# A mixer of local attention and a gated MLP on one core: new order lists for all five engines

## The chip, the core and the metric

The kernel runs on one core of one Trainium2 chip. A core has TensorE (PE in the profile; PEld is its weight load), VectorE (DVE), ScalarE (ACT), GpSimd (POOL) and SyncE (SP, which here only issues DMAs). Each works through its own list of instructions in order, and semaphores hold an instruction back until what it needs is done. The metric is the device time of one execution in microseconds (us).

## What is computed

x has 2048 rows of 512. It is layer-normalized; branch A is attention with 32 heads of 16 in which each row looks at itself and seven rows behind it, two apart; branch B is a gated MLP whose gate is mixed over the rows by a 2048 x 2048 matrix. The output is the sum of x and both.

```python
def _A_ref(x, wqkv, wo):
    B, S, D = x.shape
    H = 32
    Dh = D // H
    W, dil = (8, 2)
    qkv = (lambda x, *d: x.transpose(*d))((x @ wqkv).reshape(B, S, 3, H, Dh), 2, 0, 3, 1, 4)
    q, k, v = (qkv[0], qkv[1], qkv[2])
    scale = Dh ** (-0.5)
    pos = jnp.arange(S)
    off = jnp.arange(W) * dil
    idx = pos[:, None] - off[None, :]
    mask = idx >= 0
    ...
    logits = jnp.einsum('bhsd,bhswd->bhsw', q, kg) * scale
    logits = jnp.where(mask[None, None, :, :], logits, -1000000000.0)
    attn = _softmax(logits, axis=-1)
    o = jnp.einsum('bhsw,bhswd->bhsd', attn, vg)
    return (lambda x, *d: x.transpose(*d))(o, 0, 2, 1, 3).reshape(B, S, D) @ wo

def _B_ref(x, w_in, w_sp, b_sp, w_out):
    ...
    z = _gelu(jnp.einsum('bsd,df->bsf', x, w_in))
    z1 = z[..., :Fh].copy()
    z2 = _layernorm(z[..., Fh:], axis=-1)
    g = jnp.einsum('ts,bsf->btf', w_sp, z2) + b_sp[None, :, None]
    return jnp.einsum('bsf,fd->bsd', z1 * g, w_out)
x = A_x
xn = _layernorm(x, axis=-1)
return x + _A_ref(xn, A_wqkv, A_wo) + _B_ref(xn, B_w_in, B_w_sp, B_b_sp, B_w_out)
```

Fh is 896 here: F is 1792.

## The kernel before

The program is a set of named tasks. Each task belongs to one engine, names what it reads and writes, and holds one instruction, or on PE a run of matmuls. Waits are made from the reads and writes: a task waits for the last writer of what it reads, and for writer and readers of what it overwrites. A planner puts the tasks of each engine into a list, and `plan.orders` (L1244) gives that list by name: for each engine, each name stands behind the one before it. So the order on every engine is written out in full, and the planner's estimates have no say in it. An engine never passes over a waiting task.

The tasks, by stage. Numbers in names are blocks b of 128 rows (0 to 15), groups j of four blocks (0 to 3), weight columns c (0 to 3) or output tiles t (0 to 7, each two blocks, from the last blocks to the first).

- Normalizing x: `ldx` (a DMA, L588) brings a block into one of eight slots. `bnst` (L650) and `bnag` (L653) on DVE make mean and variance, `rstd` on POOL takes the power -0.5 (L655), `norm` on DVE applies both (L665), and `xTd` (L669, a transposing DMA issued by SP) puts the block into the transposed x, xnT. Blocks 0 to 3 are transposed on PE instead. norm of block b waits also for the transpose of block b-4, whose buffer it takes.
- q and k: `Q` and `K` (L733) on PE, 4 matmuls of 512 columns each, into a pair of PSUM banks; `QKe` (L741) on ACT evicts the pair, `halo` (L747) copies the 16 columns that the next group needs. `ldq` and `ldk` (L605) bring the weights.
- Logits: `prod` (L757) on DVE multiplies q with eight shifted k, 128 x 4096 elements; `padd` (L762) adds such products up over c. `lg` (L772) on PE sums over the 16 elements of a head with the mask hm as weights, and so waits for the last padd of its group (padd0_2 for lg0) and for hm, which POOL builds with `hm0`, `hm1`, `hm2` (L569 to L573). `lge` (L794) evicts, `smask` (L799) masks the first rows with what `mask0` and `mask1` (L576, L577) made, `pT` (L803) transposes all four groups by DMA after the last one.
- Softmax of group j: `sm1`, `sm2`, `sm3`, `ssub` (L810 to L820, DVE), `sexp` (L823, ACT), `sz1`, `sz2`, `sz3`, `srec`, `sattn` (L830 to L842, DVE).
- Branch B's halves: `z2` (L852, before it L875 for blocks 0 to 3) and `z1` (L895) on PE, 8 matmuls of 448 columns; `z2g` and `z1g` are their Gelu on ACT (L858, L882, L901). `z2s` (L907) squares z2 on ACT; DVE makes mean and variance of four blocks at a time with `zm`, `zq`, `ze`, `zv` (L915 to L924), POOL the power `zr` (L926), DVE `zb` (L928), and `zn` normalizes z2: on ACT for blocks 0 to 11 (L933), on DVE for 12 to 15 (L937). `T1` to `T4` (L954, DVE) are sums and differences of normalized blocks.
- v: `V` (L717) on PE needs the whole of xnT, `Ve` (L721) evicts on ACT.
- The mixing by w_sp in a seven-product scheme. For tile t, `w` (L962) loads the transposed weights by DMA into one of two slots, `S13`, `S2`, `S4` (L974, L978, L980, DVE) make sums of them, and `P1` to `P7` (L1015, PE) are eight matmuls of 448 columns each. `cA`, `cB`, `cE` (L1030) copy between PSUM banks on ACT, `g11` and `g21` (L1033) evict on ACT, `g12` (L1057) and `g22` (L1061) on DVE. P4 adds on into the bank that g22 reads, so P4 of a tile waits for its g22. `u` (L1039) multiplies with z1 and `uT` (L1041) transposes by DMA.
- Attention's output: `pv` (L1145), `pva` (L1149), `pvc` (L1153) on DVE, with v shifted down by partitions through `Vhaloa`, `Vhalob`, `Vzero` (L1122, L1125, DMAs), and `OTd` (L1157), a transposing DMA.
- Output: `out` (L1207 for branch A, L1211 for B, PE), `os` (L1202) and `fin` (L1220, L1219) around it, then the store.

Slot 0 of the `w` weights lies over the slots of blocks 0 to 3 and over their normalized copies, so w0_0 waits for norm8 to norm11 and w0_1 for xTd12 to xTd15 to have landed. Slot 1 lies over xnT, so w1 waits for the last V.

Of the kernel before, what the change touches and what calls it, by code (L numbers as in the profile page):

```python
# [1353 lines left out]
```

## Time and profile before

| what | value |
|---|---|
| median of 3 runs | 228.32 us (227.99 to 229.19) |
| the profiled execution, its time | 228.66 us |
| its span, first to last instruction | 226.9 us |
| mean granted TensorE clock | 1.00 |
| PE busy up to 13.15 us / from there to 125.88 / to 224.67 | 12.26 of 13.15 / 111.39 of 112.73 (DVE 111.03) / 98.75 of 98.79 |
| longest wait in total | POOL for DVE, 33.4 us in 3 waits |

A row of the profile has the start in us, the length in us, the engine, the line of the code, the operation, what it writes and reads, and how many instructions are merged in it. What stands in brackets is the time for which the engine was idle before it, and what ended that. A PE row's length holds a modelled end that reaches some 0.16 us into the next row, so that gaps on PE are read from the distance of starts. Merged rows of other engines can overlap by 0.1 us for the same reason.

### The profile page before, as it was taken

Reading aid. Unit: us, or ns where it says so; the run is one execution under the profiler, and the core shown is the slowest. Engines: PE = TensorE matmul, PEld = TensorE weight load, DVE = VectorE, ACT = ScalarE, POOL = GpSimd, SP = SyncE. Lnnn points to the kernel's source line nnn. Section 1 sums busy time; section 2 is a strip of 40 time slices with the busy share of each in tenths; the row PEclk is TensorE's granted clock in tenths of the full one; section 3 lists DMA queues with packets and bytes.
Section 4 is the critical chain, followed back from the end, with each engine's and each line's share of the span. In section 5 each row is a group of like instructions: output and inputs, shape, how many; then the busy total and the mean of one; then the engine's idle time right before and its main releaser. Section 6 shows DMA issues by size and latency. Waiting matters only on the chain.

```text
span 226.9 us, 3133 instructions
## 1 busy us (share of the span) xinstructions
PE 222.4 (98%) x1176; PEld 121.7 (54%) x1176; DVE 210.3 (93%) x255; ACT 134.2 (59%) x241; POOL 35.5 (16%) x35
## 2 busy tenths in 40 slices
...
GB/s 220 271 159 162 72 25 28 81 329 97 0 3 0 0 0 161 141 143 261 226 196 138 192 193 86 203 82 221 232 103 141 98 167 144 198 114 130 46 127 92
DMA packets 77400, 29.96 MB, mean 132 GB/s; under 512 B 68669, under 2 KB 75339, under 8 KB 77259
## 3 DMA queue, kind: packets, MB, share of 16 engines
q1 hardware_dynamic: 74250, 25.08, 53.6%
...
q8 instruction: 9, 0.15, 0.3%
...
## 4 chain that ended last, share of the span: by engine, by line
PE 44%; DVE 40%; POOL 6%; issue 5%; DMA 4%; ACT 0%; POOLq 0%; DVEq 0%
PE ps L1015 27%; DVE arena L757 13%; PE ps L1211 11%; DVE arena L762 7%; POOL fpool L655 6%; PE ps L1207 6%; DMA arena<-in_A_x_dram 4%; DVE arena L954 4%; DVE fpool L650 2%; DVE arena L1145 2%; DVE arena L974 2%; DVE arena L1149 1%; DVE arena L978 1%; DVE arena L820 1%; DVE arena L839 1%
## 5 line engine op out<-in xcount | busy, mean ns | idle before, releaser
L1015 PE MATMUL ps<-arena 128*128 128x448 f16 (+1 forms) x448 | 86.9, 353 | 0.8 <-DVE arena L978 0.7
L1015 PEld LDWEIGHTS ps<-arena 128*128 128x128 f16 (+1 forms) x448 | 43.5, 98 | 42.8 <-DVE arena L978 1.2
L757 DVE TENSOR_TENSOR arena<-arena 128x4096 bf16<-128x4096 bf16 x16 | 36.2, 2280 | 0.0
L1145 DVE TENSOR_TENSOR arena<-arena 128x4096 bf16<-128x4096 bf16 x16 | 36.0, 2277 | 0.0
L1030 ACT ACTIVATE ps<-ps 128x448 f32<-128x448 f32 x16 | 8.5, 529 | 44.4 <-PE ps L1015 25.4
L733 PE MATMUL ps<-arena 128*128 128x512 bf16 x128 | 28.5, 380 | 0.0
L1149 DVE TENSOR_TENSOR arena<-arena 128x4096 bf16<-128x4096 bf16 (+1 forms) x16 | 27.8, 1739 | 0.0
L762 DVE TENSOR_TENSOR arena<-arena 128x4096 bf16<-128x4096 bf16 x12 | 27.4, 2284 | 0.0
L1211 PE MATMUL ps<-arena 128*128 128x512 bf16 (+2 forms) x126 | 27.1, 356 | 0.0
L895 PE MATMUL ps<-arena 128*128 128x448 bf16 x128 | 24.8, 353 | 0.0
L655 POOL TENSOR_TENSOR fpool<-fpool 128x1 f32<-128x1 f32 x16 | 21.1, 1321 | 15.3 <-DVE fpool L653 14.2
L1220 ACT ACTIVATE arena<-ps 128x512 bf16<-128x512 f32 (+2 forms) x17 | 9.5, 562 | 21.1 <-PE ps L1211 21.1
L895 PEld LDWEIGHTS ps<-arena 128*128 128x128 bf16 x128 | 18.4, 145 | 6.2 <-issue 0.4
L733 PEld LDWEIGHTS ps<-arena 128*128 128x128 bf16 x128 | 14.3, 114 | 13.7 <-issue 0.8
L852 PE MATMUL ps<-arena 128*128 128x448 bf16 x96 | 19.2, 353 | 0.0
L1211 PEld LDWEIGHTS ps<-arena 128*128 128x128 bf16 x126 | 11.9, 98 | 12.4
L926 POOL TENSOR_TENSOR fpool<-fpool 128x4 f32<-128x4 f32 x4 | 12.2, 3048 | 38.5 <-DVE fpool L924 33.4
L741 ACT ACTIVATE arena<-ps 128x1024 bf16<-128x1024 f32 x16 | 16.1, 1018 | 2.5 <-PE ps L733 2.5
L1207 PE MATMUL ps<-arena 128*128 128x512 bf16 (+2 forms) x72 | 16.8, 356 | 0.0
L1033 ACT ACTIVATE arena<-ps,fpool 128x448 bf16<-128x448 f32 x16 | 10.0, 633 | 11.0 <-PE ps L1015 11.0
L907 ACT ACTIVATE arena<-arena 128x896 bf16<-128x896 bf16 x16 | 15.2, 950 | 0.1
L901 ACT ACTIVATE arena<-ps 128x896 bf16<-128x896 f32 x16 | 14.5, 922 | 0.5 <-PE ps L895 0.4
...
## 6 DMA issues: line engine op xcount, KB each, us to landing
...
arena<-arena SPq DMA_TRANSPOSE x40, 3.2
```

The costliest lines, as they stand in the source:

```text
L655: T("pool", lambda g: g.tensor_tensor(Fv("rstd", 1, b), Fv("mv", 1, 2 * b + 1), Fv("mhalf", 1), ALU.pow), reads=[("mv", b), "mhalf"], writ ...
L733: last = t.matmul(bank(k + which), AC(off["wqk"] + 1024 * dc + col0, [[4, 128]]), AC(off["xnT"] + dc * S + 512 * j, [[1, 512]]), start=(dc ...
L741: T("act", lambda a: a.activation(AC(qo, [[ko - qo, 2], [1, 512]]), ps[:, 512 * k: 512 * k + 1024].rearrange("p (t n) -> p t n", t=2), ACT ...
L757: T("dve", lambda v: v.tensor_tensor(pbv, qb, kb, ALU.mult), reads=[("QT", c, j), ("KT", c, j), ("KTpad", c, j)], writes=[("pb", s_)], est ...
L762: T("dve", lambda v: v.tensor_tensor(A("pb", 4096, 4096 * a), A("pb", 4096, 4096 * a), A("pb", 4096, 4096 * b), ALU.add), reads=[("pb", b) ...
L852: last = t.matmul(ps[:, 512 * (k + hf): 512 * (k + hf) + HF], AC(off["xnT"] + dc * S + 128 * b, [[1, 128]]), AC(off["w_in2"] + FH * dc + H ...
L895: lastm = t.matmul(ps[:, 512 * (k + hf): 512 * (k + hf) + HF], AC(off["xnT"] + dc * S + b, [[NTOK, 128]]), AC(off["w_in1"] + FH * dc + HF ...
L1015: last = t_.matmul(pb_(k_), st(k), mv(k), start=(start and k == 0), stop=(k == 7), skip_group_check=True)
L1145: T("dve", (lambda iv, tv, av: lambda v: v.tensor_tensor(tv, iv, av, ALU.mult))(iv, tv, av), reads=[("attn", q // 4)] + [("V", i_) for i_ ...
L1149: T("dve", (lambda n: lambda v: v.tensor_tensor(AC(off["Vs"], [[4096, 2], [1, n]]), AC(off["Vs"], [[4096, 2], [1, n]]), AC(off["Vs"] + n, ...
L1207: t_.matmul(po, AC(off["OT"] + 1024 * (t % 3) + 512 * r_ + 128 * cc, [[1, 128]]), AC(off["wo"] + 512 * cc + c0, [[1, n]]), start=False, st ...
L1211: last = t_.matmul(po, AC(off["z1"] + FH * tb + 128 * fc, [[1, 128]]), AC(off["w_out"] + 512 * fc + c0, [[1, n]]), start=False, stop=(fc = ...
```

## The change

All five lists in `plan.orders` are replaced; no task is added, removed or altered. On DVE the norms of blocks 8 to 15 come at other places, each with other operations between the bnag and the norm of its block, and S13_0, zv0, zb0, zn12 and zn13 stand earlier. On POOL hm0, hm1, hm2 and mask1 stand between the powers, and zr0 and zr2 come earlier. On PE and SP, the q weights and products come first; K3_3 and Q3_3 both stand ahead of lg1; P4_0 stands ahead of P1_1. On ACT the normalizations zn stand later. On SP, w0_0 and w0_1 are issued between the transposes of x, and Vhaloa behind w2_1. The lists in the diff are, in this order, those of PE, ACT, DVE, POOL and SP.

```diff
@@ -1244,60 +1244,60 @@
         plan.orders = [
             """
                 warm xTr0b fill0 xTr0a z2_0_0b z2_0_1b z2_0_0a xTr1a xTr1b z2_0_1a xNr z2_1_0a z2_1_0b z2_1_1a xTr2a
-                xTr2b z2_1_1b z2_2_0a z2_2_0b xTr3a xTr3b z2_2_1a z2_2_1b z2_3_0a z2_3_1a z2_3_1b z2_3_0b K0_0 K0_3
-                Q0_0 K0_1 Q0_1 Q0_2 K0_2 Q0_3 Q1_0 K1_0 Q1_1 K1_1 K1_2 Q1_2 K1_3 Q1_3 z2_4 z2_5 z2_6 z2_7 K2_0 K2_1
-                Q2_1 Q2_0 K2_2 Q2_2 z2_8 lg0_0 K2_3 Q2_3 z2_9 z2_10 z2_11 K3_0 Q3_0 Q3_1 K3_1 K3_2 Q3_2 K3_3 z2_12
-                z2_13 lg1_0 Q3_3 z2_15 z1_14 z2_14 z1_12 z1_15 z1_13 z1_10 z1_11 z1_8 z1_9 lg2_0 z1_6 z1_7 z1_4 z1_5
-                z1_2 z1_3 z1_0 z1_1 V14 V15 V13 V12 lg3_0 V8 V10 V6 V7 V11 V9 V4 V2 V0 V1 V5 V3 P1_0 P5_0 P6_0 P2_0
-                P7_0 P3_0 P1_1 P4_0 bits P5_1 P6_1 P2_1 P7_1 P3_1 P1_2 P4_1 P2_2 P6_2 P5_2 P7_2 P3_2 out14_0 out15_0
...
+                xTr2b z2_1_1b z2_2_0a z2_2_0b xTr3a xTr3b z2_2_1a z2_2_1b z2_3_0a z2_3_1a z2_3_1b z2_3_0b Q0_0 Q0_1
+                K0_0 Q0_2 K0_1 Q0_3 K0_3 K0_2 Q1_0 K1_0 Q1_2 Q1_1 K1_1 K1_2 Q1_3 K1_3 z2_4 z2_5 z2_6 z2_7 Q2_0 Q2_1
+                K2_1 K2_0 K2_2 Q2_2 z2_8 lg0_0 Q2_3 K2_3 z2_9 z2_10 z2_11 Q3_1 K3_1 Q3_0 K3_0 Q3_2 K3_2 Q3_3 K3_3
+                z2_12 z2_14 lg1_0 z2_13 z1_15 z2_15 z1_14 z1_10 z1_12 z1_13 z1_9 z1_11 z1_8 lg2_0 z1_6 z1_7 z1_4 z1_5
+                z1_2 z1_3 z1_0 z1_1 V14 V15 V12 V13 lg3_0 V10 V9 V11 V8 V6 V7 V4 V2 V5 V1 V0 V3 P1_0 P5_0 P6_0 P2_0
+                P7_0 P3_0 P4_0 bits P1_1 P5_1 P6_1 P2_1 P7_1 P3_1 P1_2 P5_2 P4_1 P6_2 P2_2 P7_2 P3_2 out14_0 out15_0
...
             """.split(),
             """
                 actprime ldw_in2a_1 ldw_in2b_1 ldx2 ctr0 xTe0b xTe0a xTe1a xTe1b xNe z2g0_0 xTe2a xTe2b z2g0_1 z2g1_0
-                xTe3a xTe3b z2g2_0 z2g1_1 z2g2_1 z2g3_0 z2g3_1 z2s0 QKe0_0 z2s1 QKe0_1 QKe0_2 z2s2 halo0_2 QKe0_3
-                halo0_0 QKe1_0 QKe1_1 halo0_1 halo0_3 QKe1_2 halo1_1 halo1_0 z2s3 QKe1_3 z2g4 z2s4 z2g5 z2g6 z2s5 z2g7
-                z2s6 QKe2_1 z2s7 QKe2_0 QKe2_2 z2g8 z2s8 halo1_3 QKe2_3 lge0 z2g9 halo2_1 z2g10 z2s9 z2g11 zn0 halo1_2
-                QKe3_0 QKe3_1 z2s10 QKe3_2 zn3 zn2 z2g12 z2g13 z2s11 QKe3_3 z2g15 lge1 z1g14 z2g14 zn7 z2s12 z1g15
-                z1g12 halo2_0 z1g13 zn1 z1g10 zn5 z1g11 z2s13 z1g8 z1g9 z2s14 z1g6 zn6 z1g7 halo2_2 biasf z1g4 z2s15
-                z1g5 z1g2 zn4 halo2_3 z1g3 lge2 z1g0 zn10 Ve14 z1g1 zn11 Ve12 Ve13 lge3 zn8 Ve15 Ve10 Ve6 Ve8 ldxr0
-                ldxr1 Ve7 zn9 Ve11 Ve9 Ve4 sexp3 Ve2 Ve5 cA_0 Ve3 Ve1 cB_0 Ve0 g11_0 cE_0 sexp2 cA_1 cB_1 os14_0 cE_1
...
+                xTe3a xTe3b z2g1_1 z2g2_0 z2g2_1 z2g3_0 z2g3_1 z2s0 QKe0_0 z2s1 QKe0_1 QKe0_3 halo0_3 QKe0_2 z2s2
+                halo0_2 halo0_1 QKe1_0 z2s3 QKe1_1 halo0_0 halo1_0 QKe1_2 halo1_1 QKe1_3 z2g4 z2s4 z2g5 z2g6 z2s5 z2g7
+                z2s6 QKe2_1 z2s7 QKe2_0 QKe2_2 zn0 zn2 z2g8 QKe2_3 z2s8 lge0 z2g10 z2g9 z2g11 z2s9 halo1_3 z2s10
+                QKe3_0 QKe3_1 halo2_0 z2s11 halo1_2 QKe3_3 QKe3_2 z2g12 halo2_2 halo2_1 z2g14 lge1 z2s12 z2g13 z1g15
+                z2s13 z2g15 z1g14 z2s14 z1g10 z2s15 z1g12 z1g13 zn10 zn6 z1g11 zn5 z1g8 z1g9 z1g6 zn8 z1g7 zn1 z1g4
+                z1g5 zn9 z1g2 halo2_3 z1g3 zn3 z1g0 lge2 z1g1 biasf zn11 Ve15 Ve14 Ve13 lge3 Ve10 Ve12 zn7 Ve11 ldxr1
+                Ve8 zn4 ldxr0 Ve7 Ve6 Ve9 Ve4 sexp3 Ve5 Ve2 Ve3 cA_0 Ve1 Ve0 cB_0 cE_0 g11_0 sexp2 os14_0 cA_1 os15_0
...
             """.split(),
             """
-                zeros steps0 steps1 bnst0 bnag0 ctr1 bnst1 bnag1 norm0 norm1 bnst2 bnag2 bnst3 norm2 bnag3 norm3 bnst4
-                bnag4 norm4 bnst7 bnag7 bnst5 bnag5 norm7 bnst6 bnag6 norm5 bnst9 zm0_0 norm6 bnag9 zm0 bnst10 bnst8
-                bnag10 prod0_0 bnag8 prod0_1 zq0 norm8 norm10 norm9 bnst11 bnst15 bnag11 padd0_0 norm11 bnst12 bnag15
-                prod0_2 bnst13 bnag12 bnst14 padd0_1 bnag14 bnag13 norm12 prod0_3 ze0 norm15 padd0_2 norm13 norm14
-                prod1_0 prod1_1 zv0 ze1 padd1_0 zm1 prod1_2 zb0 padd1_1 zq1 prod1_3 zv1 padd1_2 zm2 prod2_0 prod2_1
-                ze2 padd2_0 zb1 zq2 prod2_2 zm3 padd2_1 zv2 prod2_3 smask padd2_2 T3_0 prod3_0 prod3_1 zb2 padd3_0
-                T1_0 prod3_2 ze3 padd3_1 zq3 prod3_3 zv3 padd3_2 T2_0 S13_0 zn12 T4_0 zn13 zn15 zn14 T3_1 S2_0 T1_1
-                T3_3 S4_0 T2_1 sm1_3 T1_3 sm2_3 T4_1 sm3_3 T3_2 ssub3 T1_2 T2_3 T2_2 T4_3 T4_2 sz1_3 sz2_3 sz3_3 sm1_2
-                srec3 sm2_2 sattn3 sm3_2 pv15 ssub2 pv14 sz1_2 g22_0 sz2_2 S13_1 g12_0 S2_1 sz3_2 S4_1 sm1_1 pva2048_0
-                sm2_1 u14 sm3_1 pva1024_0 ssub1 srec2 g22_1 sz1_1 u15 g12_1 sz2_1 pvc0 sattn2 S13_2 S2_2 sz3_1 u12
...
-                g12_6 pva2048_6 S2_7 pva1024_6 u3 pvc6 u2 pv1 pv0 S4_7 pva2048_7 g22_7 pva1024_7 pvc7 g12_7 u0 zb3 u1
-                fin1_1
+                zeros steps0 steps1 bnst0 bnag0 ctr1 bnst1 bnag1 norm0 norm1 bnst2 bnag2 bnst3 norm2 bnag3 norm3 bnst5
+                bnag5 bnst6 norm5 bnag6 bnst7 bnag7 norm6 bnst4 bnag4 norm7 norm4 zm0_0 bnst8 zm0 bnst9 bnag8 zq0
+                bnag9 bnst10 prod0_0 prod0_1 bnag10 norm8 bnst11 norm9 bnag11 padd0_0 ze0 norm10 zv0 bnst13 bnst12
+                norm11 bnag13 bnag12 bnst14 prod0_2 bnst15 zb0 padd0_1 bnag15 bnag14 norm12 prod0_3 norm13 padd0_2
+                norm14 prod1_0 norm15 prod1_1 ze1 padd1_0 zm1 prod1_2 zq1 padd1_1 zm2 prod1_3 S13_0 padd1_2 zq2 ze2
+                prod2_0 prod2_1 zv2 padd2_0 zv1 prod2_2 zm3 padd2_1 zb2 prod2_3 zb1 padd2_2 zq3 prod3_0 prod3_1 ze3
+                padd3_0 zv3 prod3_2 smask padd3_1 zn13 prod3_3 zn12 padd3_2 zn14 S2_0 zn15 T3_0 T3_3 T3_2 T1_0 T1_3
+                T1_2 T2_0 S4_0 T2_2 sm1_3 sm2_3 T4_2 sm3_3 T3_1 ssub3 T2_3 T1_1 T4_3 T2_1 T4_0 sz1_3 T4_1 sz2_3 sz3_3
+                sm1_2 srec3 sm2_2 sattn3 sm3_2 pv14 pv15 g22_0 ssub2 S13_1 g12_0 sz1_2 S2_1 sz2_2 pva2048_0 sz3_2
+                sm1_1 u14 pva1024_0 sm2_1 S4_1 u15 sm3_1 pvc0 ssub1 S13_2 g22_1 srec2 sz1_1 g12_1 S2_2 sz2_1 u12 sm1_0
...
+                pv2 g12_6 pva2048_6 S13_7 pva1024_6 S2_7 u3 pvc6 u2 pv1 pv0 S4_7 pva2048_7 g22_7 pva1024_7 pvc7 g12_7
+                zb3 u0 u1 fin1_1
             """.split(),
             """
-                mhalf ident0 ident1 nident0 nident1 ktpad rstd0 rstd1 rstd2 rstd3 rstd4 mask0 hm0 hm1 rstd7 rstd5
-                rstd6 hm2 rstd9 rstd10 rstd8 rstd11 mask1 rstd15 rstd12 rstd13 rstd14 zr0 zr1 zr2 zr3
+                mhalf ident0 ident1 nident0 nident1 ktpad rstd0 rstd1 rstd2 rstd3 mask0 rstd5 rstd6 rstd7 rstd4 rstd8
+                rstd9 hm0 rstd10 rstd11 zr0 hm1 rstd12 rstd13 rstd14 hm2 rstd15 zr2 mask1 zr1 zr3
             """.split(),
             """
-                ldx0 ldx1 ldw_in2a_0 ldw_in2b_0 ldx3 ldx4 ldx7 ldx5 ldx6 ldk ldq ldx9 ldx8 ldx10 xTd4 xTd7 xTd5 xTd6
-                ldx11 ldx15 ldx13 ldx14 ldx12 xTd10 xTd8 ldb xTd9 xTd11 xTd15 xTd12 xTd13 xTd14 ldwv ldw_in1 w0_0 w0_1
-                ldwout pT3 pT2 pT0 pT1 w1_0 w1_1 Vhaloa w2_0 w2_1 Vhalob ldwo0 Vzero ldwo2 ldwo3 ldwo1 uT14 OTd0 uT15
-                w3_0 w3_1 uT12 w4_0 uT13 w4_1 OTd1 uT10 w5_0 uT11 OTd2 w5_1 w6_0 uT8 uT9 OTd3 w6_1 w7_0 uT7 w7_1 OTd4
-                uT6 uT4 OTd5 uT5 uT3 OTd6 uT2 OTd7 uT0 uT1 st7_1_192 st7_1_0
+                ldx0 ldx1 ldw_in2a_0 ldw_in2b_0 ldx3 ldx6 ldx5 ldx7 ldx4 ldq ldk ldx8 ldx9 ldx10 xTd5 xTd6 xTd4 xTd7
+                ldx11 ldx15 ldx13 ldx12 ldx14 xTd8 xTd9 ldb xTd10 xTd11 xTd12 w0_0 xTd14 xTd13 xTd15 w0_1 ldw_in1 ldwv
+                ldwout pT3 pT2 pT0 pT1 w1_0 w1_1 Vhalob ldwo3 ldwo1 Vzero w2_0 w2_1 Vhaloa ldwo0 ldwo2 uT14 OTd0 uT15
+                w3_0 w3_1 uT12 w4_0 OTd1 uT13 w4_1 uT10 uT11 w5_0 w5_1 OTd2 w6_0 uT8 uT9 w6_1 OTd3 uT6 OTd4 uT7 w7_0
+                w7_1 uT5 OTd5 uT4 uT2 uT3 OTd6 OTd7 uT0 uT1 st7_1_192 st7_1_0
             """.split(),
         ]
         plan.schedule(**(sched_kw or {}))
```

More of the change, by code (lines that the diff above doesn't have):

```diff
@@ new lines, in build_kernel @@
+                Ve8 zn4 ldxr0 Ve7 Ve6 Ve9 Ve4 sexp3 Ve5 Ve2 Ve3 cA_0 Ve1 Ve0 cB_0 cE_0 g11_0 sexp2 os14_0 cA_1 os15_0
+                cB_1 g21_0 g11_1 cE_1 sexp1 cA_2 os12_0 cE_2 g21_1 cB_2 fin14_0 g11_2 cA_3 g21_2 os13_0 sexp0 ldxr2
+                g11_3 cB_3 fin12_0 fin15_0 ldxr3 cE_3 cA_4 st0_0_0 cB_4 g11_4 fin13_0 os11_0 os8_0 cE_4 os10_0 g21_3
+                st1_0_0 g21_4 cA_5 fin10_0 os9_0 fin11_0 st2_0_0 cB_5 ldxr4 cE_5 g11_5 cA_6 cB_6 os6_0 fin8_0 g21_5
+                fin9_0 ldxr5 cE_6 os7_0 fin7_0 g11_6 os4_0 st3_0_0 fin6_0 os5_0 ldxr6 g21_6 cA_7 st4_0_0 ldxr7 fin5_0
@@ L1272, in build_kernel @@
+                cB_7 fin4_0 st5_0_0 os0_0 cE_7 g11_7 os2_0 g21_7 os3_0 fin2_0 os1_0 fin3_0 os1_1 fin0_0 os1_2 st6_0_0
+                fin1_0 st7_0_0 fin1_2 st7_1_384
             """.split(),
             """
[L1274 to L1276 removed]
@@ L1282, in build_kernel @@
-                srec3 sm2_2 sattn3 sm3_2 pv15 ssub2 pv14 sz1_2 g22_0 sz2_2 S13_1 g12_0 S2_1 sz3_2 S4_1 sm1_1 pva2048_0
-                sm2_1 u14 sm3_1 pva1024_0 ssub1 srec2 g22_1 sz1_1 u15 g12_1 sz2_1 pvc0 sattn2 S13_2 S2_2 sz3_1 u12
-                S4_2 sm1_0 u13 pv12 pv13 g12_2 pva2048_1 sm2_0 g22_2 pva1024_1 u10 S13_3 pvc1 S2_3 sm3_0 pv10 srec1
-                ssub0 S4_3 pv11 g22_3 pva2048_2 S13_4 u11 g12_3 S2_4 sz1_0 pva1024_2 S4_4 pvc2 u8 pv8 pv9 u9 pva2048_3
-                g22_4 pva1024_3 g12_4 sattn1 u6 S13_5 pvc3 S2_5 sz2_0 pv6 pv7 sz3_0 S4_5 pva2048_4 srec0 pva1024_4
```

17 lines of the change are left out of this document (7 added, 10 removed).

## The prediction

> **What bounds the kernel now.** I read the page's busy shares first, then the chain of work that ended last, then TensorE's (PE's) instructions in order of time for every place where it stood still, then VectorE (DVE) and GpSimd (POOL) side by side.
>
> ```profile
> PE 222.4 (98%) x1176; PEld 121.7 (54%) x1176; DVE 210.3 (93%) x255; ACT 134.2 (59%) x241; POOL 35.5 (16%) x35
> ```
> ```profile
> 125.13 0.70 DVE arena L978
> 125.83 0.05 issue
> 125.88 6.23 PE ps L1015 x32
> ```
> The chain is DVE up to 125.83 us and PE without a break from there. Both are nearly full all the time, so an edit can win only what PE stands still. PE in order of time:
>
> ```profile
> 52.72 3.27 PE L852 MATMUL ps<-arena 128*128 128x448 bf16 x16
> 56.27 0.61 PE L772 MATMUL ps<-arena 128*32 128x512 bf16 x8 [0.28 <-DVE arena L762]
> ...
> 89.51 0.62 PE L772 MATMUL ps<-arena 128*32 128x512 bf16 x8 [0.24 <-DVE arena L762]
> ...
> 125.88 6.23 PE L1015 MATMUL ps<-arena 128*128 128x448 f16 x32 [0.74 <-DVE arena L978]
> 136.69 12.27 PE L1015 MATMUL ps<-arena 128*128 128x448 bf16 x64
> 148.80 1.03 PE L1207 MATMUL ps<-arena 128*128 128x512 bf16 x4
> ```
> The last two rows give PE's pace: 64 matmuls of 448 columns from 136.69 to 148.80, 0.189 each, so a gate product of eight is 1.513. Against it PE lost 0.42 before lg1 (52.72 + 16 x 0.189 + 0.10, the 0.10 being what lg0 also shows, is 55.85, not 56.27), some 0.31 before lg3, and 1.18 in the gates between 100.48 and 125.88 (25.40 for sixteen products, 24.2 by the pace). These 1.9 us are the most there is to win; after 125.88 there is no gap.
>
> DVE stands still only here, after the start:
>
> ```profile
> 22.27 1.05 DVE L665 TENSOR_SCALAR arena<-arena,fpool 128x512 bf16<-128x512 bf16 x3 [0.44 <-POOL fpool L655]
> ...
> 27.23 0.43 DVE L665 TENSOR_SCALAR arena<-arena,fpool 128x512 bf16<-128x512 bf16 x1 [0.44 <-POOL fpool L655]
> ...
> 34.35 2.28 DVE L757 TENSOR_TENSOR arena<-arena 128x4096 bf16<-128x4096 bf16 x1
> ...
> 39.75 0.41 DVE L665 TENSOR_SCALAR arena<-arena,fpool 128x512 bf16<-128x512 bf16 x1 [0.19 <-POOL fpool L655]
> ```
> These are norm8, norm11 and norm14, each waiting for its power on POOL. The cause is in POOL's rows:
>
> ```profile
> 17.39 2.50 POOL L655 TENSOR_TENSOR fpool<-fpool 128x1 f32<-128x1 f32 x1 [0.77 <-DVE fpool L653]
> ...
> 31.29 0.55 POOL L655 TENSOR_TENSOR fpool<-fpool 128x1 f32<-128x1 f32 x1 [0.37 <-DVE fpool L653]
> 34.22 2.85 POOL L655 TENSOR_TENSOR fpool<-fpool 128x1 f32<-128x1 f32 x1 [2.38 <-DVE fpool L653]
> 37.03 2.61 POOL L655 TENSOR_TENSOR fpool<-fpool 128x1 f32<-128x1 f32 x1
> 44.72 3.07 POOL L926 TENSOR_TENSOR fpool<-fpool 128x4 f32<-128x4 f32 x1 [5.07 <-DVE fpool L922]
> ```
> A power takes 0.55 alone, but one that meets a 2.2 us prod or padd ends 0.42 after that ends. The one at 31.29, 0.41 ahead of a padd (31.70), passed; the one at 34.22, only 0.13 ahead of a prod (34.35), was held.
>
> **The change, part by part**, in times of the profiled execution, with each operation by the distance of starts in its row: prod and padd 2.17 to 2.21, bnst 0.60, norm 0.33, bnag and the 128x4 operations 0.10, S13 1.14, S2 and S4 0.60, T 0.54, zn on DVE 0.42.
>
> *Start.* q weights now land first, k second; PE's first group needs only the first load in both orders and its third needs the second, so 13.15 stays (bounds 0 and the second load's issue distance, 0.5; I take 0, for the bytes are the same). The norms of x4 to x7 end by about 14.4 instead of 15.9, and their transposes leave no later. Then x8's arrival (14.81 in the row of the first bnst after it) rules as x9's did: three bnst and four small operations give 17.1 for prod0_0, which QKe0_0 (15.98 + 1.02) allows. It was 17.23: 0.1 won.
>
> *To lg0.* From prod0_0 to the end of padd0_2 took 21.93 (17.23 to 39.16). The set of operations is the same but for two more small ones and one less. Minus 0.88 of waits, plus 0.1: 21.16, so 38.3. No norm is now due before its power: rstd8 to rstd11 end at the latest 0.42 after a prod that has another operation behind it. The power's own lateness then falls under that operation.
>
> *To lg1.* norm14 and norm15 0.66, four small 0.45, S13_0 (moved ahead from 89.9) 1.14, seven of 2.21: 17.7, so padd1_2 ends at 56.0 (56.13 before). S13_0 needs both w0 loads; w0_1 leaves SP after xTd15 has landed (41.2 + 2.4 to 4.5 by the rows of these transposes) and takes 4.6 to 7.9 by its own line, 48 to 53.6 against 52.6: 0, at worst 1.0. PE comes to lg1 one weight group later (0.87, since Q3_3 and K3_3 both stand ahead), at 56.7. DVE is 0.7 early: the 0.42 goes.
>
> *To lg2.* Same count of operations as before, 16.2: 72.2. PE: 56.7 + 0.55 + ten groups of 1.513 + 0.1 = 72.5. No wait.
>
> *To lg3.* 17.05 less T3_0 and T1_0 (1.08) plus zn12, zn13 (0.84): 16.8, so 89.0, and lg3 0.14 later as before, 89.1; PE is there at 88.7 and still waits 0.4. Against 89.51: **0.4 won**.
>
> *Gates.* P1_0 starts 0.55 + 10.42 after lg3, at 100.1. DVE from padd3_2 to the first pv took 15.87; without S13_0, zn12, zn13, with T3_0, T1_0: 14.97, so 103.9. Then pv14, pv15 (4.4), g22_0 (0.6): 108.9. P4_0 now follows P3_0 at once (P1_1 stood between), due at 100.1 + 6 x 1.513 = 109.2: 0.2 in hand. S4_1, S13_2 and S2_2 come at 117.6, 120.6 and 123.6 by adding the rows in the new order; PE wants them at 118.2, 121.3 and 124.3. So the **1.18** goes too, with 0.6 or 0.7 in hand.
>
> *ACT.* Eight of its zn (1.03 each) now stand among the z1 groups and two among the V. The rows put zn6 at 69.7 while zb1 comes at 70.0: 0.3 of waiting, covered by the bank that z1_7 wants, 0.75 later. At nothing; without that cover 0.3.
>
> *SP.* Vhaloa now goes behind w2_1, which waits for P4_0. It leaves at about 113 and lands 9.2 later, at 122; transposes behind such a copy are held till it lands (w2_0's issue took 7.3 behind it). uT14, OTd0, uT15, w3_0, w3_1 follow one by one, the last landed at 133; pv13 wants Vhaloa at 126, S13_3 wants w3_1 at 136.6. Hidden by some 4 us.
>
> *Tail.* DVE ends with u1 at 216.5; it gains its 0.9 + 0.2 + 0.1 of waits, about 1.1. out0 waits for uT0, which landed at 215.95 + 3.1, 0.6 ahead of out0 (219.66). So PE can gain up to 1.7 before DVE's end binds. It gains **0.4 + 1.18 = 1.58**: span 226.9 to 225.3, and the profiled 228.66 to 227.1. That execution lay 0.34 above the median of the runs, 228.32, so 226.75; two places have 0.2 or less in hand, for which I add 0.15: **226.9**.
>
> **The rivals.**
>
> *H: hm2 gets in POOL's way.* It was done at 14.73; now it stands between rstd14 and rstd15. rstd14 starts at 33.4, 0.2 ahead of prod0_3, nearer to the 0.13 that was held than to the 0.41 that passed, so it ends at 36.3, and hm2 falls under padd0_2 (to 38.3). No row has such a select beside a prod; the nearest, mask1 at 27.16 beside a norm, took 0.35. If it is held, rstd15 starts with prod1_0 and ends at 41.4; norm15, at 40.9, waits 0.5, and lg3 comes at 89.6. Won: 1.18 - 0.1 = 1.08, time 227.25. The Trainium skill, "SBUF — State Buffer", section "Who interferes with whom", says that a VectorE instruction with two SBUF inputs contends with a GpSimd instruction that reads SBUF, and that the first to issue keeps the port; that is H, since a select reads. On the order the trace differs, if its starts are to be trusted: the power at 34.22 began before the prod at 34.35 and still took 2.85.
>
> *M: the waits move.* The three margins of 0.6 to 0.7 in the gates are sums of some thirty operations; if what is worth 1.18 there comes back as a wait at S13_2, S2_2 or P5_3, only lg3's 0.4 stays: 227.9. For it: before, DVE was behind at just these products. Against: DVE is 1 us earlier there.
>
> *S: slower.* P4_0 has lost its cover. In before g22_0 ran at 110.58, with P1_1 in between, and PE lost only 0.26. If DVE's gain doesn't reach g22_0 and it starts at 111.2, 0.65 later than in before, P4_0 starts at 112.0 instead of 109.2. PE then loses 2.8: -0.4 + 2.8 - 1.18 = 1.2 slower, 229.5. It decides from an end of g22_0 later than 109.1, and costs one for one. Against it: DVE must lose 2.9 against my sum, of which norm15 gives 0.5, S13_0 held for w0_1 1.0, and the rest would have to come from sm1_3 (95.4), whose transposed logits by the longest landing of L803 (4.5 after lge3's end at 90.7) are only just there.
>
> That the norms are not behind their powers can be excluded by the lists.
>
> **How the numbers follow.** Forecast 0.40 (226.9), H 0.18 (227.25), M 0.24 (227.9), S 0.18 (229.5). A measurement can tell about 0.5% from no change, 1.14 us: below 227.2 is faster, above 229.45 slower. H lies on that line, half each: faster 0.49, same 0.33, slower 0.18. The range goes from 226.3 (all 1.9 won, and 0.1) to 229.4, with most of S left out; the forecast's own is 226.4 to 227.4.
>
> **What would show it.** Right: no wait of L665 for POOL after 17 us; lg1 without a wait; lg3 near 89.1; no PE gap between 100 and 126, and the first L1207 near 130.5 instead of 131.94. H: norm15 waits 0.5 and POOL's select lasts over 1 us. M: PE waits for L974 or L978. S: PE waits for L1061 near 109. I am wrong if PE waits over 1 us at any place, or if DVE waits for a DMA.

## The result and the profile after

The changed kernel takes 226.92 us (median of 7 runs, 226.64 to 227.14), the kernel before, beside it, 228.13 (7 runs, 227.87 to 229.21). The ratio is 0.9944, 95% interval 0.9928 to 0.996. The profiled execution took 226.93, its span is 225.2 (before: 228.66 and 226.9). The busy shares on the page of the changed kernel:

```profile
PE 219.8 (98%) x1163; PEld 121.4 (54%) x1176; DVE 209.9 (93%) x255; ACT 135.6 (60%) x241; POOL 35.4 (16%) x35
```
No work has gone: DVE's 209.9 us are the 210.3 of before, and PE's 219.8 are less than the 222.4 of before because this trace lacks the records of 13 matmuls (x1163 against x1176). What has gone is time in which PE stood still. PE of the changed kernel in order of time:

```profile
12.63 13.76 PE L733 MATMUL ps<-arena 128*128 128x512 bf16 x62
26.22 6.22 PE L852 MATMUL ps<-arena 128*128 128x448 bf16 x32
...
55.93 0.61 PE L772 MATMUL ps<-arena 128*32 128x512 bf16 x8
...
72.09 0.61 PE L772 MATMUL ps<-arena 128*32 128x512 bf16 x8 [0.31 <-DVE arena L762]
...
88.95 0.61 PE L772 MATMUL ps<-arena 128*32 128x512 bf16 x8 [0.53 <-DVE arena L762]
89.50 10.58 PE L717 MATMUL ps<-arena 128*128 128x512 bf16 x47
99.92 10.76 PE L1015 MATMUL ps<-arena 128*128 128x448 bf16 x56
110.51 0.19 PE L1193 MATMUL ps<-arena 128*128 128x64 bf16 x1
110.54 19.84 PE L1015 MATMUL ps<-arena 128*128 128x448 bf16 x104
130.43 0.81 PE L1207 MATMUL ps<-arena 128*128 128x512 bf16 x3
```
Three things are to be read here. PE begins q and k (L733) at about 12.4, not at 13.15: the row starts at 12.63, but it has 62 of 64 matmuls, and the 64 took 13.84 us in the kernel before (13.16 to 27.00), which leads back from 26.22 to 12.38. lg1 waits no more, but lg2 and lg3 do: from 55.93 to 72.09 are 16.16 us, of which 0.55 for lg1, ten groups of 1.513 and 0.1 make 15.78, so 0.38 is lost there, and 0.59 before lg3 (16.86 from lg2, where a run below without a wait has 16.27). And from 99.92 on there is no gap: 160 matmuls and the small one end where the first out begins. (The row at 130.43 lacks one matmul's record, having 3 of 4, so that out began one matmul earlier, at 130.21; it was 131.94.)

What holds lg2 and lg3 is seen in the chain that ended last. Between DVE's operations it goes over POOL for one stretch (start, length, what):

```profile
32.70 2.81 POOL fpool L655
35.51 2.19 POOL arena L573
37.70 2.87 POOL fpool L655
```
and in the rows behind it, POOL's and then DVE's:

```profile
26.19 0.21 POOL L570 TENSOR_SCALAR_AFFINE_SELECT arena<-arena 128x32 bf16<-128x32 bf16 x1
...
32.70 2.81 POOL L655 TENSOR_TENSOR fpool<-fpool 128x1 f32<-128x1 f32 x1 [2.71 <-DVE fpool L653]
35.48 2.22 POOL L573 TENSOR_SCALAR_AFFINE_SELECT arena<-arena 128x32 bf16<-128x32 bf16 x1
37.68 2.88 POOL L655 TENSOR_TENSOR fpool<-fpool 128x1 f32<-128x1 f32 x1
```
```profile
35.35 2.28 DVE L762 TENSOR_TENSOR arena<-arena 128x4096 bf16<-128x4096 bf16 x1
...
37.87 2.28 DVE L757 TENSOR_TENSOR arena<-arena 128x4096 bf16<-128x4096 bf16 x1
40.60 0.41 DVE L665 TENSOR_SCALAR arena<-arena,fpool 128x512 bf16<-128x512 bf16 x1 [0.44 <-POOL fpool L655]
```
hm2 (L573), a select of 128x32, lasts 2.22 us beside padd0_2 (35.35 to 37.55); hm1 (L570), a select of the same size with no large DVE operation beside it, lasts 0.21. rstd15 stands behind hm2, is caught by prod1_0 in turn, and norm15 waits 0.44 for it. This is the mechanism of rival H. Its 0.44 us are about what DVE had won at the start (prod0_0 at 16.61, where 17.1 was forecast), which the prediction had not seen either.

The gates, on DVE: the rows that P4_0, P5_2 and P6_2 wait for.

```profile
108.08 0.68 DVE L1061 SCALAR_TENSOR_TENSOR arena<-ps,fpool 128x448 bf16<-128x448 f32 x1
...
119.22 1.22 DVE L974 TENSOR_TENSOR arena<-arena 128x2048 f16<-128x2048 bf16 x1
...
122.68 0.69 DVE L978 TENSOR_TENSOR arena<-arena 128x1024 f16<-128x1024 f16 x1
```
S2_2 (L978) starts 2.45 us earlier than before (125.13). PE comes to P6_2 after sixteen products, at 99.92 + 16 x 1.513 + 0.03 = 124.16. In the kernel before, PE went on 0.75 after the start of this row (125.88 against 125.13), which here is 123.43: 0.73 to spare.

### The profile page after: what moved, and what is told of

The parts are those of the page before. It is cut to its first block, busy times and chain, and to the rows that moved or that the text cites. A ratio compares the mean times of both kernels' runs of the same rounds, so it can differ in the third digit from the quotient of the medians.

```text
span 225.2 us, 3128 instructions
## 1 busy us (share of the span) xinstructions
PE 219.8 (98%) x1163; PEld 121.4 (54%) x1176; DVE 209.9 (93%) x255; ACT 135.6 (60%) x241; POOL 35.4 (16%) x35
## 4 chain that ended last, share of the span: by engine, by line
PE 59%; DVE 29%; issue 5%; POOL 5%; DMA 1%; ACT 0%
PE ps L1015 38%; DVE arena L757 12%; PE ps L1211 11%; DVE arena L762 8%; PE ps L1207 6%; PE ps L717 5%; POOL fpool L655 4%; DVE fpool L650 4%; DVE arena L665 2%; DVE fpool L653 1%; DMA arena<-in_A_x_dram 1%; POOL arena L573 1%; DVE arena L974 1%; PE ps L772 0%; DVE arena L937 0%
## 5 line engine op out<-in xcount | busy, mean ns | idle before, releaser
L733 PE MATMUL ps<-arena 128*128 128x512 bf16 x124 | 27.8, 379 | 0.2
L1211 PE MATMUL ps<-arena 128*128 128x512 bf16 (+2 forms) x125 | 26.9, 355 | 0.1
L655 POOL TENSOR_TENSOR fpool<-fpool 128x1 f32<-128x1 f32 x16 | 19.9, 1249 | 14.8 <-DVE fpool L653 12.8
L733 PEld LDWEIGHTS ps<-arena 128*128 128x128 bf16 x128 | 14.4, 113 | 13.3 <-issue 0.4
L1211 PEld LDWEIGHTS ps<-arena 128*128 128x128 bf16 x126 | 11.9, 98 | 12.4
L1207 PE MATMUL ps<-arena 128*128 128x512 bf16 (+2 forms) x66 | 15.5, 353 | 0.3
L926 POOL TENSOR_TENSOR fpool<-fpool 128x4 f32<-128x4 f32 x4 | 10.1, 2530 | 30.9 <-DVE fpool L924 30.8
```

What stands on the lines that cost most here:

```text
L655: T("pool", lambda g: g.tensor_tensor(Fv("rstd", 1, b), Fv("mv", 1, 2 * b + 1), Fv("mhalf", 1), ALU.pow), reads=[("mv", b), "mhalf"], writ ...
L733: last = t.matmul(bank(k + which), AC(off["wqk"] + 1024 * dc + col0, [[4, 128]]), AC(off["xnT"] + dc * S + 512 * j, [[1, 512]]), start=(dc ...
L1207: t_.matmul(po, AC(off["OT"] + 1024 * (t % 3) + 512 * r_ + 128 * cc, [[1, 128]]), AC(off["wo"] + 512 * cc + c0, [[1, n]]), start=False, st ...
L1211: last = t_.matmul(po, AC(off["z1"] + FH * tb + 128 * fc, [[1, 128]]), AC(off["w_out"] + 512 * fc + c0, [[1, n]]), start=False, stop=(fc = ...
```

## The experiments

Every kernel was run beside the kernel before on the same chip. Most compare orders only, so a diff shows the pieces of lists that move. Two theories of the gates run through them: L, that the gates waited only because DVE came to them late, and O, that they need their new order.

**e1_new_head: the new lists up to lg3, the old ones behind it.** To join them, ACT's order between lge3 and sexp3 was written anew, with zn7 ahead of Ve12; among the T, those with 1 and 2 behind the underscore are exchanged, here and in e2.

```diff
 DVE  ... padd3_1 zn13 prod3_3 zn12 padd3_2
-     zn14 S2_0 zn15 T3_0 T3_3 T3_2 ... pv14 pv15 g22_0 ssub2 S13_1 ...
+     T3_0 T1_0 T2_0 T4_0 zn15 zn14 ... pv15 ssub2 pv14 sz1_2 g22_0 ...
 PE   ... lg3_0
-     V10 V9 ... P3_0 P4_0 bits P1_1 ...
+     V8 V10 ... P3_0 P1_1 P4_0 bits ...
```


> The new lists up to padd3_2, lg3 and lge3, the old order behind them (T_1 and T_2 of groups 1 and 2 exchanged, since zn4 and zn7 are now the late ones). Theory L (DVE's lead): DVE reaches the gates with 0.65 us from the first half and 0.9 us less work left (S13_0, zn12, zn13 done, T3_0 and T1_0 still to do), so the first pv comes 1.55 earlier than in before and S2_2 ends at 124.3; PE wants it at 124.1, the gap at P6_2 shrinks from 0.74 to about 0.2: some 1.5 us below before, ratio 0.993 to 0.995. Rival O (the order of the gates does it): the gaps of 1.18 stay, only lg3's 0.56 is won: ratio 0.9975.

Measured: 227.65 (11 runs, 227.31 to 228.24), ratio 0.9981 (0.9971 to 0.9991). PE's rows:

```profile
92.12 8.86 PE L717 MATMUL ps<-arena 128*128 128x512 bf16 x40 [0.76 <-ACT arena L721]
100.82 12.27 PE L1015 MATMUL ps<-arena 128*128 128x448 bf16 x64
...
131.11 1.03 PE L1207 MATMUL ps<-arena 128*128 128x512 bf16 x4
```
The joint cost PE about 1.0 us in the V, which is an accident of the experiment. But the old gate order then ran through without a gap (30.29 us from 100.82 to 131.11, as in the changed kernel), which speaks for L. Since PE came late, it is not yet a clean answer.

**e2_new_tail: the old lists up to lg3, the new ones behind it.** The same, the other way round.

```diff
 DVE  ... zq3 prod3_3 zv3 padd3_2
-     T2_0 S13_0 zn12 T4_0 zn13 zn15 ... pv15 ssub2 pv14 sz1_2 g22_0 ...
+     S13_0 zn13 zn12 zn14 S2_0 zn15 ... pv14 pv15 g22_0 ssub2 ...
```


> The old lists up to padd3_2, lg3 and lge3, the new order behind them. Theory L: DVE has no lead and 0.9 us more to do; g22_0 ends near 110.8 and P4_0, which follows P3_0 at once, is due at 109.6, so PE waits 0.7 to 1.2 there: 0 to 0.5 us below before, ratio 0.998 to 1.000. Rival O: the gates run without a gap, 1.1 us below before, ratio 0.995. The rival on the slower side that was on record (P4_0 without cover) would show as a wait for L1061 near 110.

Measured: 228.41 (11 runs, 228.04 to 228.62), ratio 1.001 (1.0002 to 1.0019). The joint on ACT cost more here:

```profile
91.69 9.72 PE L717 MATMUL ps<-arena 128*128 128x512 bf16 x44 [1.20 <-ACT arena L721]
```
Nothing was won. The gates themselves ran without a gap (30.30 us from 101.24 to 131.54), but with 1.4 us of its own making in front of them this run can't tell the theories apart. An estimate from its rows leans to L: g22_0 starts at 109.11 and P4_0 can follow 0.74 later; without the 1.4 us PE would have been due there at 108.9 and would have waited some 0.9.

**e3_masks_early: the changed kernel with the four masks back ahead of the powers.**

```diff
 POOL ... rstd3 mask0
-     rstd5 rstd6 rstd7 rstd4 rstd8 rstd9 hm0 rstd10 rstd11 zr0 hm1 rstd12 rstd13 rstd14 hm2 rstd15 zr2 mask1 ...
+     hm0 hm1 hm2 mask1 rstd5 rstd6 rstd7 rstd4 rstd8 rstd9 rstd10 rstd11 zr0 rstd12 rstd13 rstd14 rstd15 zr2 ...
```


> The changed kernel with hm0, hm1, hm2 and mask1 ahead of rstd5 on POOL, nothing else. Theory H (hm2 under padd0_2 made rstd15 late): norm15 no longer waits 0.44, lg2 comes without a wait, lg3 at 88.5, and the end moves by the same 0.4: 226.5, ratio to before 0.9925. Rival: the 0.44 is lost anyway (rstd15 is held by the next padd or prod whatever stands ahead of it), the time stays at 226.9.

Measured: 226.54 (5 runs, 226.23 to 226.79), ratio 0.993 (0.9919 to 0.9942). On POOL, and on PE:

```profile
32.84 2.82 POOL L655 TENSOR_TENSOR fpool<-fpool 128x1 f32<-128x1 f32 x2 [2.71 <-DVE fpool L653]
```
```profile
71.93 0.62 PE L772 MATMUL ps<-arena 128*32 128x512 bf16 x8
...
88.55 0.62 PE L772 MATMUL ps<-arena 128*32 128x512 bf16 x8 [0.29 <-DVE arena L762]
```
Neither power is held under padd0_2, norm15 starts at 40.22 without a wait, lg2 does not wait, lg3 comes 0.40 earlier, and so does the first out (129.81). H is shown, with its price. This kernel is the best that was run, by point estimate; its interval and that of the change overlap.

**e4_norms_only: the kernel before with three names moved on DVE.**

```diff
 DVE  ... zq0
-     norm8 norm10 norm9 bnst11 bnst15 bnag11 padd0_0 norm11 bnst12 ... norm13 norm14 prod1_0 ...
+     bnst11 norm8 norm10 norm9 bnst15 bnag11 padd0_0 bnst12 norm11 ... norm13 prod1_0 norm14 ...
```


> The kernel before with three moves on DVE alone: bnst11 ahead of norm8, norm11 behind bnst12, norm14 behind prod1_0. Theory L: DVE's waits of 0.44, 0.44 and 0.19 go, lg1 comes without a wait, lg3 0.7 earlier (PE is then the later one), S2_2 1.07 earlier, so 1.0 us below before, ratio 0.9955. Rival O: lg3's part alone, 0.3 to 0.5 us, ratio 0.998 to 0.9985, since the gates keep the order that made PE wait.

Measured: 227.53 (12 runs, 226.97 to 229.79), ratio 0.9984 (0.9965 to 1.0003). The runs fall into two groups: six between 226.97 and 227.25, which is what L asks for, and six between 227.81 and 229.79. The profiled execution, at 229.79, is the slowest of the second kind; the other five of it were not profiled. It shows, on PE and in SP's queue:

```profile
121.19 10.76 PE L1015 MATMUL ps<-arena 128*128 128x448 bf16 x56 [1.30 <-DMA arena<-in_B_w_sp_dram]
```
```profile
91.20 11.79 SPq L803 DMA_TRANSPOSE arena<-arena  x4
...
108.08 0.66 SPq L1122 DMA_DIRECT2D arena<-arena  x1
108.84 11.65 SPq L962 DMA_TRANSPOSE arena<-in_B_w_sp_dram  x2
```
In SP's rows the length is how long the issuing took. The four pT took 11.8 us here (8.4 in before, 8.2 in the changed kernel); w1 came late by that, and w2 (108.84) stood behind Vhaloa (108.08), a copy of 1.5 MB, for 11.65. P1_2 had to wait for it. A second wait follows in the same way: DVE waits 1.82 for the loads that S13_3 reads (w3), and PE 0.77 for S13_3 at 140.49.

**e5_old_gates: the changed kernel up to the end of V, the old gate order on PE, ACT and DVE behind it, SP as changed.** This is e1 without the accident on ACT.

```diff
 PE   ... V3 P1_0 P5_0 P6_0 P2_0 P7_0 P3_0
-     P4_0 bits P1_1 P5_1 P6_1 P2_1 P7_1 P3_1 P1_2 P5_2 P4_1 P6_2 P2_2 ...
+     P1_1 P4_0 bits P5_1 P6_1 P2_1 P7_1 P3_1 P1_2 P4_1 P2_2 P6_2 P5_2 ...
 DVE  ... sm3_2
-     pv14 pv15 g22_0 ssub2 S13_1 g12_0 ...
+     pv15 ssub2 pv14 sz1_2 g22_0 sz2_2 S13_1 g12_0 ...
```


> The changed kernel up to the end of V (so P1_0 at 99.9 as there, and DVE with the lead that it has there), but behind that the old order of the gate stage on PE, ACT and DVE (pv15 ahead of pv14, P1_1 ahead of P4_0, two sz between the products of S); SP keeps the new order. Theory L (the gate stage of before waited only because DVE entered it late; the lead of about one us is what carries it): 226.9 +-0.3, PE without a gap from 99.9 to 130.2, first L1207 matmul at about 130.4. Theory O (the new order behind P1_0 is needed, as the prediction's 1.18 us of the gates has it): P4_1 or P1_2 waits for DVE as before, 1.2 us lost, 228.1, first L1207 at 131.6.

Measured: 229.47 (6 runs, 229.34 to 230.92), ratio 1.0072 (1.0051 to 1.0094). Neither time came. PE's rows say why:

```profile
100.28 12.27 PE L1015 MATMUL ps<-arena 128*128 128x448 bf16 x64
...
112.41 18.51 PE L1015 MATMUL ps<-arena 128*128 128x448 f16 x96
130.97 0.81 PE L1207 MATMUL ps<-arena 128*128 128x512 bf16 x3
...
165.22 0.81 PE L1207 MATMUL ps<-arena 128*128 128x512 bf16 x3 [2.10 <-DMA arena<-arena]
```
In the gates PE loses 0.2 at most, where O asks for 1.2: S2_2 starts at 123.94, PE is due at P6_2 at 100.28 + 24.24 = 124.52, and it goes on 0.75 after that start. So L holds, though with nothing to spare. The loss of the run is 35 us later and has another cause: an out (out10) waits for a transposing DMA. By SP's rows that is OTd2, issued at 159.89; in SP's new list it stands behind w5_1, whose issue took 4.27, and in the old list ahead of it, as the old lists of DVE and PE want it.

**e6_old_sp: the changed kernel with SP's old order behind pT1.**

```diff
 SP   ... pT3 pT2 pT0 pT1 w1_0 w1_1
-     Vhalob ldwo3 ldwo1 Vzero w2_0 w2_1 Vhaloa ldwo0 ldwo2 uT14 OTd0 uT15 w3_0 w3_1 uT12 w4_0 OTd1 uT13 ...
+     Vhaloa w2_0 w2_1 Vhalob ldwo0 Vzero ldwo2 ldwo3 ldwo1 uT14 OTd0 uT15 w3_0 w3_1 uT12 w4_0 uT13 w4_1 OTd1 ...
```


> The changed kernel with SP's old order behind the four pT alone (w2_0 and w2_1 behind Vhaloa, all ldwo behind Vhalob, the old places of uT, OTd, w3 to w7). Theory L: PE comes to the gates 0.5 us ahead of before and w2 lands when it did (its issue was held from 106.8 to 117.3 there), so no wait: 226.9 +-0.3. Theory D (the new place of w2, ahead of Vhaloa, carries part of the gain): PE waits at L1015 for w2 near 121, as it did in the run of norms one later, 1.3 us there: 227.5 to 228.2, and the times spread over more than 1 us.

Measured: 230.1 (7 runs, 228.82 to 231.78), ratio 1.0071 (1.0041 to 1.0101). Both theories missed. In the profiled execution (231.78, the slowest of the seven) there was no wait for w2 near 121, but

```profile
145.22 1.49 PE L1207 MATMUL ps<-arena 128*128 128x512 bf16 x3 [2.90 <-DMA arena<-arena]
```
The changed PE asks for out12 before P7_3, and the old SP issues OTd1, which out12 reads, two places later; another out loses 1.05 in the same way near 195. The wait also cost more than itself: the granted clock was 0.50 from 145 to 148, and the first matmuls of out12 started 0.43 us apart, not 0.216: some 1.4 us lost beside the changed kernel's rows for the same work; after the 2.10 us of e5 nothing of the kind is seen. e5 and e6 say the same from two sides: the lists of SP and of the engines behind the gates were made for each other, and half of a set cost 2.5 and 3.2 us in the medians.

**e7_k_first: the changed kernel with k ahead of q again.**

```diff
 SP   ... ldx4
-     ldq ldk
+     ldk ldq
 PE   ... z2_3_0b
-     Q0_0 Q0_1 K0_0 Q0_2 K0_1 Q0_3 K0_3 K0_2
+     K0_0 K0_3 Q0_0 K0_1 Q0_1 Q0_2 K0_2 Q0_3
```


> The changed kernel with the k weights loaded ahead of the q weights again, and PE and ACT in the old order over group 0 (K0_0 K0_3 Q0_0 K0_1 ...). My theory: the start differs from one execution to the next by the clock that PE has in its first matmuls and not by this order, so 226.9 +-0.3, QK at 12.6 and prod0_0 at 16.6 in the profile. Rival Q (the order of q and k is what won 0.5 us at the start): 227.4, QK at 13.1 and prod0_0 at 17.1 or later.

Measured: 226.99 (6 runs, 226.76 to 227.74), ratio 0.9952 (0.9938 to 0.9967). PE's rows:

```profile
13.03 8.58 PE L733 MATMUL ps<-arena 128*128 128x512 bf16 x39
22.09 5.37 PE L733 MATMUL ps<-arena 128*128 128x512 bf16 x23 [0.47 <-ACT arena L741]
```
PE loses 0.47 at 22.09. It then comes to lg2 and lg3 later, where it had waited for DVE, and waits there no longer. The start lies between the two expectations, 13.03 by the row (two of its records are missing too) and prod0_0 at 16.79. The time stays; the order of q and k is worth nothing that can be measured.

**e8_masks_bnst8: e3 with bnst8 ahead of norm4.**

```diff
 DVE  ... norm7
-     norm4 zm0_0 bnst8 zm0
+     bnst8 norm4 zm0_0 zm0
```


> The kernel with the four masks early on GpSimd (226.54 before) and on DVE bnst8 ahead of norm4, so that norm4's wait of 0.44 us for its power at 14.2 is filled. Theory: DVE's chain from there to padd3_2 moves 0.3 to 0.4 us forward (QKe0_0 ends at 16.4 and allows prod0_0 no earlier), the wait of 0.3 before lg3 goes, and PE, which then waits nowhere, wins that 0.3: 226.2 to 226.3. Rival: x block 8 has not landed at 13.8 and bnst8 waits: 226.5 or more, with a DMA named behind L650.

Measured: 226.64 (5 runs, 226.48 to 226.89), ratio 0.9934 (0.9922 to 0.9946). norm4's wait went, but prod0_0 started at 16.75 as it had (16.76), and at lg3 ACT now binds:

```profile
88.54 0.61 PE L772 MATMUL ps<-arena 128*32 128x512 bf16 x8 [0.22 <-ACT arena L721]
```
Neither theory: no transfer was late, and the wait removed was covered.

**e9_norms_w2: e4, and on SP w2 ahead of Vhaloa.**

```diff
 SP   ... w1_0 w1_1
-     Vhaloa w2_0 w2_1 Vhalob ldwo0
+     Vhalob w2_0 w2_1 Vhaloa ldwo0
```


> The kernel before with two things alone taken from the change: on DVE bnst11 ahead of norm8, norm11 behind bnst12 and norm14 behind prod1_0 (as in the run of norms one later), and on SP w2_0 and w2_1 with the small Vhalob ahead of the large Vhaloa. Everything else, the gate order, the q/k order and GpSimd's list, is the old one. Theory L (the change's gain is DVE's lead, and w2 must not stand behind the large copy): PE has no gap at L1015 and the times lie together at 227.0 to 227.3, without the second group at 227.8 to 229.8. Theory O (the gate order is needed too): 227.8 to 228.2.

Measured: 227.17 (8 runs, seven of them 227.03 to 227.53, one 228.23), ratio 0.9964 (0.995 to 0.9977). SP's queue and PE:

```profile
90.40 11.51 SPq L803 DMA_TRANSPOSE arena<-arena  x4
...
108.00 6.25 SPq L962 DMA_TRANSPOSE arena<-in_B_w_sp_dram  x2
```
```profile
88.27 0.62 PE L772 MATMUL ps<-arena 128*32 128x512 bf16 x8
...
99.23 12.27 PE L1015 MATMUL ps<-arena 128*128 128x448 bf16 x64
...
124.31 6.23 PE L1015 MATMUL ps<-arena 128*128 128x448 f16 x32 [0.67 <-DVE arena L978]
130.37 1.03 PE L1207 MATMUL ps<-arena 128*128 128x512 bf16 x4
```
The four pT are as late as in e4 (11.5), and no wait for w2 follows. Five names moved bring the first out to within 0.16 us of the changed kernel (130.37 against 130.21). The way there differs: S13_0, zn12 and zn13 are still behind padd3_2, so lg3 comes 0.68 earlier, at 88.27; then S2_2 comes 0.88 later, at 123.56, and PE gives 0.67 back. The change, which puts this work ahead of lg3, moves the wait from the one place to the other and wins nothing net. That it is the work, and not the gate order, which takes the 0.67 away is seen in e5: there the old gate order follows the moved work, and 0.2 at most is left.

**e10_g22_later: the changed kernel with g22_0 behind S13_1.** This prices rival S.

```diff
 DVE  ... pv14 pv15
-     g22_0 ssub2 S13_1 g12_0
+     ssub2 S13_1 g22_0 g12_0
```


> The changed kernel with g22_0 behind S13_1 on DVE: it ends at 110.5 in place of 108.76, and P4_0, which PE reaches at 109.0 straight behind P3_0, waits for its bank. My theory (the changed order has about 0.2 us to spare there, and nothing behind it takes the loss up): 1.5 us lost, 228.4. Rival (slack further on, as the next products of S are then made 0.6 us sooner against PE, takes it up): under 227.4.

Measured: 228.73 (12 runs, 228.35 to 229.1), ratio 1.002 (1.001 to 1.0029).

```profile
110.77 1.69 PE L1015 MATMUL ps<-arena 128*128 128x448 f16 x8 [1.39 <-DVE arena L1061]
```
P4_0, due at 100.14 + 6 x 1.513 = 109.22, starts at 110.77: 1.55 lost there, 1.8 in the median. Nothing takes it up.

**e11_g22_cover: the same, with P1_1 between P3_0 and P4_0.**

```diff
 PE   ... P7_0 P3_0
-     P4_0 bits P1_1
+     P1_1 P4_0 bits
```


> The same with g22_0 behind S13_1, and on PE P1_1 put between P3_0 and P4_0, as it stood before the change. My theory: P4_0 is reached at 110.5, when g22_0 has just ended, so nearly the whole 1.5 us is covered: 226.9 to 227.1. Rival (P1_1's own bank or its mover is late there): 228 or more.

Measured: 226.97 (6 runs, 226.56 to 227.4), ratio 0.9948 (0.9934 to 0.9961); no gap in the gates. One product of cover is worth the whole of it.

**e12_hm2_behind: the changed kernel with hm2 behind rstd15.**

```diff
 POOL ... rstd14
-     hm2 rstd15
+     rstd15 hm2
```


> The changed kernel with one name moved: hm2 behind rstd15 on GpSimd, not between rstd14 and rstd15. Theory H (it is this one small operation, held under padd0_2, that makes norm15 late): rstd15 follows rstd14 at 35.4 within 0.1 us, norm15 starts without a wait at 40.2, lg2 and lg3 move 0.4 us forward, 226.5 +-0.2, as with all four masks moved. Rival (another mask or the sum of them held GpSimd up): 226.9, norm15's wait stays.

Measured: 227.73 (12 runs, 227.15 to 229.44), ratio 0.9984 (0.9961 to 1.0007). By the medians it is worse than with hm2 ahead. POOL, then PE:

```profile
32.65 5.34 POOL L655 TENSOR_TENSOR fpool<-fpool 128x1 f32<-128x1 f32 x2 [2.71 <-DVE fpool L653]
37.96 2.23 POOL L573 TENSOR_SCALAR_AFFINE_SELECT arena<-arena 128x32 bf16<-128x32 bf16 x1
```
```profile
40.33 0.61 PE L772 MATMUL ps<-arena 128*32 128x512 bf16 x8 [1.19 <-POOL arena L573]
```
norm15 doesn't wait, as H says. But rstd15 was held under padd0_2 and hm2 under prod1_0, to 40.19, and lg0, which has hm as its weights, waits 1.19 for it. The expectation had overlooked that lg0 is due at 39.1. Of two operations that are each held for one large DVE operation, the second is late whichever it is; of the places tried for hm2, only the one of e3, ahead of the powers, helps. At the end the profiled execution (227.21, the second fastest of the twelve) is only 0.3 behind the changed kernel, since the waits at lg2 and lg3 fall away; what the slower executions lost is not on record.

## Why the prediction was right, and where by luck

The time is 226.92 against 226.9, and the forecast's own signs came: lg1 and the gates without a wait, about 0.5 won at lg3. Both signs of rival H came with them (norm15 waited 0.44, the select lasted 2.22), though H's time was 227.25. Two errors on DVE, of half a microsecond each and of opposite sign, are hidden in the number, and that they cancel is luck. By its steps:

- *Start: 13.15 stays, prod0_0 at 17.1.* Wrong as to the size. PE began q and k at about 12.4, prod0_0 started at 16.61. On PE the change didn't do this: the old order of the start shows 12.54 (e2), 12.68 (e9) and 13.45 (e4), and e7, with k first in the changed kernel, 13.03. It differs from one execution to the next. In the profiled execution of before the first six matmuls of L875 took 1.94 us, in that of the changed kernel 1.31. The error was to set the sum against one execution's start as if it belonged to the kernel. For prod0_0 a part may be the change's: it starts at 16.52 to 16.97 in the ten profiles with DVE's new start, the changed kernel's among them, and at 16.88 to 17.52 in the four with the old one; no run moves that piece of the list alone. That x8's arrival rules prod0_0 was wrong too: bnst8 started at 14.54 without a wait.
- *To lg0, "no norm is now due before its power".* Wrong for norm15, by H, which had a chance of its own and 0.5 as its price: 0.44 was measured, and e3, without it, lies 0.38 lower in the median.
- *lg1: the 0.42 goes.* Right. *lg2: no wait.* Wrong, 0.38: PE came 0.8 earlier than the sum had it (lg1 at 55.93, not 56.7), and DVE had given back at norm15 most of what it won at the start. *lg3: 89.1, 0.4 won.* 88.95, 0.56 won: the 0.4 with the start's 0.5 more and norm15's 0.44 less would be 0.46.
- *Gates: 1.18 goes.* Right, and with the margins that the sum gave: P4_0 0.2 predicted and 0.18 measured (108.08 + 0.74 by e10's rows, against 109.0), P5_2 and P6_2 0.6 to 0.7 predicted, 0.73 measured for P6_2. But the reason was narrower than the text had it. In e1 and e5 the old order runs with no gap over 0.2 as well, once DVE leads PE; what the new order adds is margin, 0.73 at P6_2 where e5 has none. And the 0.67 that e9 still loses, and that the work put ahead of lg3 takes away, is lost again at lg3.
- *Sum: 1.58 won.* 1.73 at the first out and 1.7 in the span, from one profiled execution to the other. In the medians it is 1.21, where the forecast had 1.42 (228.32 to 226.9): the kernel before, run again beside the changed one, had its median at 228.13, and its profiled execution lay 0.53 above that. The 0.15 added for places with little in hand was not lost at any of them.
- *ACT and SP at nothing; Vhaloa leaves at about 113; the tail doesn't bind.* Right: Vhaloa left at 113.62, no wait for a DMA behind it, and u1 ended at 214.8 with PE dense to the end. That transposes behind such a copy are held till it lands was too strong: uT14's issue was over at 120.9, and the copy landed 9.9 after its issue, at 123.5. That w2 ahead of Vhaloa protects against late pT was not seen; e4 and e9 show it.
- *Rival S.* Its mechanism is as priced, one for one and from an end of g22_0 at about 109 (e10), and so is the cover (e11). Its condition, that DVE's gain doesn't reach g22_0, was not met.
- *Rival M.* None of the three products waited.

On H the Trainium skill, "SBUF — State Buffer", section "Who interferes with whom", had said beforehand that a VectorE instruction with two SBUF inputs contends with a GpSimd one that reads SBUF: the trace agrees, 2.22 us for the select beside padd0_2 against 0.21. Of the start, the skill's page "TensorE: Matmul & The Clock Gate", section "Part 1: The HAM clock gate (the "warmup" mystery)", says that the window in which a cold PE becomes fast is not tied to the kernel's start, so that the number of slow matmuls changes from run to run. The 1.94 and 1.31 us for the same six matmuls agree with that: the slow ones of before start 0.35 to 0.37 us apart, the others 0.19. But the profile's granted clock reads 1.00 there in both, so the trace does not show that the clock is the cause, and no run here set the window on purpose.

Open: why the four pT take 7.3 us to issue in one execution and 11.8 in another; and why rstd14, starting 0.13 us ahead of prod0_3, passed in e3 (0.62, so that only rstd15 was held, 2.23), while with a lead of 0.11 in e12 and 0.12 in the changed kernel it was held itself (2.82 and 2.81), as was the power with 0.13 in before (2.85).
